# Expert products of a gated recurrence with top-k routing on one core: column halves of 64, an expert's lag, and longer weight runs

## The chip, the cores and the metric

One core of one Trainium2 chip. The metric is the device time of one execution in microseconds (us); lower is better. The kernel before was run three times: median 218.14 us, 217.22 to 218.26.

## What is computed

A gated linear recurrence over 5056 steps, 4 batches and 256 channels makes 20224 tokens. Each token goes to the best of 8 experts; an expert keeps its 80 tokens with the highest gate weight and runs a two-layer product on them. All other rows of the output are zero.

```python
sig = 1.0 / (1.0 + np.exp(-f_logit))
f = lower_bound + (1.0 - lower_bound) * sig
for t in range(S):
    h = f[:, t] * h + (1 - f[:, t]) * x[:, t];  y[:, t] = h
x = y.reshape(B * S, D)
...
logits = x @ w_gate;  expert_idx = argmax(logits);  gate_w = max(softmax(logits))
for e in range(E):
    tok_idx = tokens of e; if more than capacity = 80, the 80 with the largest gate_w
    out[tok_idx] = gate_w[tok_idx, None] * (np.maximum(x[tok_idx] @ w1[e], 0.0) @ w2[e])
```

w1 is 8 x 256 x 1024 and w2 8 x 1024 x 256, all float32.

## The kernel before

It has three stages, and one queue, SP's, issues nearly all transfers in program order.

**Recurrence.** 40 units of 512 steps and one batch each. SP loads f_logit and x of a unit (`load`, L251 and L253, 512 KB each, runs of 4 KB), ACT takes the sigmoid (L257), POOL multiplies (L261), PE turns both to channels by transposes (`to_channels`, L268), ACT makes the decay (`decay`, L278), DVE scans (`scan`, L286). The result stays on chip as `h_all`. PE also forms the gate logits (`logits`, L301): weights of 32 columns, four matmuls on the four quarters of the array, each written to its own 32 partitions of PSUM. After four units of a group ACT, PE and DVE turn the logits to tokens and take maxima (L310 to L346).

**Selection.** From the last units on: exponentials on ACT (`exponentials`, L355; the first one over all eight older groups, 1024 columns), sums by halves on POOL (`halved`, L369), the worth of each token (L379, L383), transposes and copies to candidates (`candidates`, L389 and L395), the peaks on DVE (L400). Then two small copies on ACT (L487 the last 256 candidates, L490 the last peaks), the maxima of each row on DVE (L560 to L563), ranks, and 12 matmuls (L626) that put the kept tokens in slots. `trow` holds where they lie.

**Experts.** `experts` (from L664) runs over the 8 experts. `gather` (L688 to L693) copies the 80 tokens of an expert from `h_all`, two channels at a time, on DVE, ACT and POOL together; `scaled` (L701) scales them on DVE. The weights come in 32 tiles of 512 KB, four per expert, through a ring of six (`wring`): `weights` loads a half of W1 by hidden columns (L514, two runs of 2 KB per partition) or a half of W2 by hidden rows (L518, four runs of 1 KB). The order of the tiles is sorted by the step at which they are used (`e_step`). When a tile has been used, `more` issues the next and, behind it, one clear. A clear (`clear`, L169) copies a block of zeros inside the output, DRAM to DRAM, 256 KB mostly; 22 of the 76 quarter blocks are left when the ring is full, so each of the next 22 tiles has one behind it and the last four of the 32 have none. At most eight of SP's transfers are under way, as eight semaphores take turns.

`steps` walks over 64 chunks of 128 hidden columns: `hidden` (L725) makes two matmuls for a chunk (stationary a 128 x 128 block of W1, moving the 80 tokens), and `result` (L740), six chunks later, one for the second product (stationary the 80 tokens' hidden values of a chunk, moving 256 columns of W2), accumulated over eight chunks into 80 x 256, token by row. `relu` (L734) on ACT moves four chunks at a time from PSUM. `finish` (L755) scales by the gate weight on DVE, and `scatter` (L758) on POOL writes the 80 rows to the output by an indirect transfer. Scatters wait in a list until all clears are issued; the first then waits for the clears to land.

## Time and profile before

| | |
|---|---|
| runs | 218.14 us median (217.22 to 218.26) |
| profiled execution | 217.36 us, its span 215.5 us |
| busy | PE 187.8, weight loads 158.2, DVE 150.7, ACT 131.4, POOL 139.1 us |
| moved | 80.55 MB, mean 374 GB/s; SP's queue 94.9% of the 16 engines' span |
| w_sb transfers | 32 of 512 KB, median 7.7 us from issue to landing |
| granted TensorE clock | 0.992 over the span |

The span begins with the first instruction and ends with the last; the execution's own time has some 1.9 us around it. Busy shares are means over stages with different limits, so the rows further down are taken by stretch. PEld is the weight load that goes ahead of a matmul. A matmul in f32 has two records in the trace, a transpose one. A DMA share is the mean busy share of the 16 DMA engines; it can stand a little above 1, since packets of an engine overlap.

### The profile page before, as it was taken

How to read it: one execution, taken by the hardware profiler on the slowest of the kernel's cores; microseconds unless marked ns; L12 is line 12 of the kernel's file. 1: busy time of each engine (PE TensorE's matmuls, PEld its weight loads, DVE VectorE, ACT ScalarE, POOL GpSimd, SP SyncE). 2: the span in 40 equal slices, each digit the busy share in tenths (PEclk: the TensorE clock that was granted, in tenths of full speed). 3: DMA queues.
4: the chain of work that ended last, by engine and by line, in shares of the span. 5: the costliest groups of instructions: out<-in, count | busy, mean ns of one | idle time of the engine just before them, and what ended most of it. 6: DMA issues, size and time to landing. Idle time of an engine off the chain costs nothing. (4 is left out here: it accounts for less than half of the span.)

```text
span 215.5 us, 5581 instructions
## 1 busy us (share of the span) xinstructions
PE 187.8 (87%) x1878; PEld 158.2 (73%) x1878; DVE 150.7 (70%) x479; ACT 131.4 (61%) x370; POOL 139.1 (65%) x279
## 2 busy tenths in 40 slices
PE   7888689999999999999999767798969899889980
PEld 7677478788878787878788546798857687668850
DVE  5687659999998989898989768945777524510010
ACT  4776588879888888888878623559524443611100
POOL 3484887989898989898888761049966623000741
PEclk9999999999999999999999999999999999999996
DMA  6999999999999999999999899999999999999910
GB/s 218 414 399 416 417 422 415 418 414 426 409 417 414 419 411 417 411 407 424 409 408 395 283 378 363 386 320 400 338 368 410 392 406 405 404 401 397 319 57 24
DMA packets 28825, 80.55 MB, mean 374 GB/s; under 512 B 3058, under 2 KB 11380, under 8 KB 26484
## 3 DMA queue, kind: packets, MB, share of 16 engines
q1 hardware_dynamic: 28400, 79.45, 94.9%
q0 software_dynamic: 384, 0.66, 1.0%
q8 instruction: 17, 0.28, 0.5%
q14 instruction: 20, 0.16, 0.2%
q10 hardware_dynamic: 4, 0.00, 0.0%
HBM read 78.39 MB, written 21.36 MB: 463 GB/s over the span
## 5 line engine op out<-in xcount | busy, mean ns | idle before, releaser
L261 POOL TENSOR_TENSOR x_t<-f_t,x_t 128x1024 f32<-128x1024 f32 x39 | 92.3, 2374 | 16.4 <-DMA x_t<-in_x_dram 11.0
L286 DVE TENSOR_TENSOR_SCAN h_all<-h_all,up 128x512 f32<-128x512 f32 (+1 forms) x80 | 94.7, 1242 | 7.5 <-ACT h_all L278 6.5
L278 ACT ACTIVATE h_all<-sp,nomlb 128x512 f32<-128x512 f32 (+1 forms) x80 | 50.0, 676 | 12.6 <-PE sp L268 12.5
L257 ACT ACTIVATE f_t<-f_t 128x1024 f32<-128x1024 f32 x40 | 42.4, 1061 | 9.3 <-DMA f_t<-in_f_logit_dram 9.2
L268 PE MATMUL up<-ident,x_t 128*128 128x128 f32 x320 | 42.0, 274 | 4.7 <-POOL x_t L261 4.7
L725 PEld LDWEIGHTS h_ps<-xt,w_sb 128*128 128x128 f32 x256 | 36.8, 191 | 12.5 <-DVE xt L701 3.5
L268 PE MATMUL sp<-ident,f_t 128*128 128x128 f32 x320 | 44.6, 283 | 0.1
L268 PEld LDWEIGHTS sp<-ident,f_t 128*128 128x128 f32 x320 | 35.0, 143 | 8.2 <-issue 5.5
L268 PEld LDWEIGHTS up<-ident,x_t 128*128 128x128 f32 x320 | 35.6, 141 | 6.8 <-POOL x_t L261 6.7
L725 PE MATMUL h_ps<-xt,w_sb 128*128 128x80 f32 x256 | 36.8, 269 | 4.0 <-DMA w_sb<-in_moe_w_dram 3.1
L740 PE MATMUL y_ps<-w_sb,hid 128*80 128x256 f32 x128 | 37.3, 381 | 1.3 <-DMA w_sb<-in_moe_w_dram 1.3
L693 POOL COPY xe<-h_all 128x8 uint8 x192 | 26.5, 198 | 16.4 <-issue 6.5
L301 PE MATMUL lg<-h_all,wg 128*32 128x128 f32 (+1 forms) x640 | 26.5, 282 | 5.3 <-ACT ls L310 3.9
L693 DVE COPY xe<-h_all 128x8 uint8 x256 | 20.8, 163 | 11.5 <-issue 11.4
L734 ACT ACTIVATE hid<-h_ps 128x320 f32<-128x320 f32 x16 | 7.0, 436 | 32.3 <-PE h_ps L725 32.3
L301 PEld LDWEIGHTS lg<-h_all,wg 128*32 128x32 f32 x640 | 15.4, 108 | 12.3 <-ACT ls L310 6.8
L693 ACT COPY xe<-h_all 128x8 uint8 x192 | 20.2, 193 | 5.5 <-issue 3.5
L758 POOL DMA_INDIRECT out_dram<-y,goal x8 | 7.5, 938 | 23.8 <-DMA w_sb<-in_moe_w_dram 19.7
L755 DVE TENSOR_SCALAR y<-y_ps,gsl 80x256 f32<-80x256 f32 x8 | 3.8, 477 | 22.6 <-PE y_ps L740 22.6
L183 PE MATMUL warm<-ident 128*128 128x128 f32 x128 | 17.2, 298 | 1.4 <-POOL ident masks.py:199 1.4
L183 PEld LDWEIGHTS warm<-ident 128*128 128x128 f32 x128 | 16.6, 212 | 1.5 <-POOL ident masks.py:199 1.4
L740 PEld LDWEIGHTS y_ps<-w_sb,hid 128*80 128x80 f32 x128 | 14.8, 152 | 2.2 <-issue 1.4
(126 smaller groups left out, 91.9 us busy)
## 6 DMA issues: line engine op xcount, KB each, us to landing
f_t<-in_f_logit_dram SPq DMA_DIRECT2D x40, 512.0 KB, 6.1
x_t<-in_x_dram SPq DMA_DIRECT2D x40, 512.0 KB, 6.5
w_sb<-in_moe_w_dram SPq DMA_DIRECT2D x32, 512.0 KB, 7.7
out_dram<-out_dram SPq DMA_DIRECT2D x34, 256.0 KB, 7.8
out_dram<-out_dram SPq DMA_DIRECT2D x6, 768.0 KB, 11.6
out_dram<-out_dram SPq DMA_DIRECT2D x4, 1024.0 KB, 12.4
out_dram<-zero SPq DMA_DIRECT2D x4, 256.0 KB, 8.4
out_dram<-out_dram SPq DMA_DIRECT2D x2, 512.0 KB, 7.8
```

The lines of the kernel that those rows point to most:

```text
L183: nc.tensor.matmul(warm, ident, ident, start=True, stop=True)
L257: nc.scalar.activation(s_t, s_t, ACT.Sigmoid, scale=-1.0)
L261: (nc.gpsimd if n else nc.vector).tensor_tensor(u_t, sts[n], u_t, ALU.mult)
L268: nc.tensor.transpose(at, src[n][:, r, ds(o * P, P)], ident)
L278: nc.scalar.activation(columns(n, o).rearrange("c (p r) -> c p r", r=R), sps.pop((n, o)).rearrange("c (r p) -> c p r", r=R) [:, lead(n // ...
L286: nc.vector.tensor_tensor_scan(h, h, ups.pop((n, o))[:, lead(n // B):], columns(n - B, o)[:, size(n // B - 1) - 1:] if n >= B else 0.0, AL ...
L301: nc.tensor.matmul(lgs[g][ds(r * LC, LC), b, :k], wg[:, o], h[:, r], start=o == 0, stop=o == DC - 1, skip_group_check=True)
L693: copy(xe[:, :, ds(WORD * (k + j), WORD)], pair(v - HOME))
L725: nc.tensor.matmul(HP[e, i][:, c], w[1, e, i][:, o, ds(c * P, P)], XT[e][:, o], start=o == 0, stop=o == DC - 1, skip_group_check=True)
L734: nc.scalar.activation(HID[e][:, ds(i * CH, CH)], HP.pop((e, i)), ACT.Relu)
L740: nc.tensor.matmul(YP[e], HID[e][:, c], w[2, e, c // CH][:, c % CH], start=c == 0, stop=c == FC - 1)
L758: one = nc.gpsimd.indirect_dma_start(out=out, out_offset=bass.IndirectOffsetOnAxis(ap=goal[:, ds(e, 1)], axis=0), in_=Y.pop(e), in_offset= ...
```

## The change

Six edits. W1 is loaded by halves of the 256 input channels, one run of 4 KB per partition, and `hidden(e, o)` uses one such half for all eight chunks. W2 is loaded with two hidden rows next to each other on a partition, two runs of 2 KB; so that the hidden values match, `hidden` takes every second column of W1. Each matmul of `hidden` has 64 stationary columns, two of them for the two halves of the partitions. `result` is turned: W2 is stationary, 64 output channels at a time, and the hidden values move, so that the product comes out by channel; `lift` copies it from PSUM on ACT and `across` turns it to tokens by two transposes on PE. The second product of an expert runs between the two input halves of the next; the transposes, `finish` and `scatter` come one expert later still. In the selection, the first exponential is cut in two and group 8's is taken earlier and to a tile of its own, its sum goes ahead of its choice, and the two small ACT copies stand behind the first maximum (L560) and its replacement. Pools are opened without `with` (the routing code moves one level to the left), `gsm` on the right side, and the weights of the ring stand ahead of the end of the selection in the program.

```diff
-def e_step(key, chunks, half, lag):
+def e_step(key):
     which, e, i = key
-    return e * chunks + i * half + (lag if which == 2 else 0), which
+    return 2 * (e + which - 1) + i, which
...
         elif n == LAST - 2:
-            exponentials(0, OLD)
+            exponentials(0, HALF)
         elif n == LAST - 1:
             halved(0, HALF)
+            exponentials(HALF, OLD)
+            exponentials(OLD, OLD + 1, aside=True)
...
     aside(g, 0, B - 1)
-    best = chosen(OLD)
-    exponentials(OLD, OLD + 1)
     logits(LAST)
     aside(g, B - 1, B)
+    sums(OLD, OLD + 1)
+    best = chosen(OLD)
     worth(0, 0, 2, nc.gpsimd)
     worth(2, 0, 2, nc.gpsimd)
     mark(OLD, *best, nc.gpsimd)
-    sums(OLD, OLD + 1)
...
     peaks(HALF, fresh)
-    nc.scalar.copy(cand[:, OLD * P:], fresh[:, NP * TOP:])
-    eighths = fresh[:, TOP - 1:NP * TOP:TOP]
-    last_of = consts.tile([P, NP], F32, name="last_of")
-    nc.scalar.copy(last_of, eighths)
+    gsm.release()
...
         nc.vector.match_replace(out=rest, in_to_replace=vals2[:, :TOP], in_values=fresh,
                                 imm_value=GONE)
+        nc.scalar.copy(cand[:, OLD * P:], fresh[:, NP * TOP:])
+        last_of = consts.tile([P, NP], F32, name="last_of")
+        nc.scalar.copy(last_of, fresh[:, TOP - 1:NP * TOP:TOP])
...
     def weights(which, e, i):
-        t = wring.tile([P, DC * FH], F32, name="w_sb", tag="w_sb")
+        t = wring.tile([P, F], F32, name="w_sb", tag="w_sb")
         if which == 1:
-            t = t.rearrange("p (o f) -> p o f", o=DC)
-            nc.sync.dma_start(out=t, in_=w1[e][:, ds(i * FH, FH)].rearrange(
-                "(o p) f -> p o f", p=P))
+            nc.sync.dma_start(out=t, in_=w1[e][ds(i * P, P)])
         else:
             t = t.rearrange("p (c d) -> p c d", c=CH)
-            nc.sync.dma_start(out=t, in_=w2[e][ds(i * FH, FH)].rearrange(
-                "(c p) d -> p c d", p=P))
+            nc.sync.dma_start(out=t.rearrange("p (h j) d -> p h j d", j=RUN),
+                              in_=w2[e][ds(i * FH, FH)].rearrange(
+                                  "(h p j) d -> p h j d", p=P, j=RUN))
...
+            def hidden(e, o):
+                if o == 0:
+                    for i in range(2):
+                        HP[e, i] = psh.tile([P, CH, K], F32, name="h_ps", tag="h_ps")
+                for c in range(FC):
+                    i, c = divmod(c, CH)
+                    h, r = divmod(c, RUN)
+                    for j in range(0, P, HC):
+                        at = i * FH + (h * P + j) * RUN + r
+                        nc.tensor.matmul(HP[e, i][ds(j, HC), c],
+                                         w[1, e, o][:, at:at + (HC - 1) * RUN + 1:RUN],
+                                         XT[e][:, o], start=o == 0 and c == 0,
+                                         stop=o == DC - 1, skip_group_check=True)
+                del w[1, e, o]
+                more(1)
...
+            def result(e, i):
+                if i == 0:
+                    both = psy.tile([P, 2 * D], F32, name="y_ps", tag="y_ps")
+                    YP[e] = both[:, :DC * K].rearrange("p (o k) -> p o k", o=DC)
+                    YZ[e] = both[:K, D:]
+                for c in range(CH):
+                    for o in range(DC):
+                        for j in range(0, P, HC):
+                            nc.tensor.matmul(YP[e][ds(j, HC), o],
+                                             w[2, e, i][:, c, ds(o * P + j, HC)],
+                                             HID[e][:, i * CH + c],
+                                             start=i == 0 and c == 0 and o == 0,
+                                             stop=i == 1 and c == CH - 1, skip_group_check=True)
+                del w[2, e, i]
+                more(1)
+
+            def lift(e):
+                YC[e] = mp.tile([P, DC, K], F32, name="yc", tag="yc", bufs=1)
+                nc.scalar.copy(YC[e], YP.pop(e))
+
+            def across(e):
+                yc = YC.pop(e)
+                for o in range(DC):
+                    nc.tensor.transpose(YZ[e][:, ds(o * P, P)], yc[:, o], ident)
...
             for e in range(E):
                 gather(e + 2, (0,))
+                hidden(e, 0)
+                if e > 1:
+                    across(e - 2)
+                if e > 0:
+                    result(e - 1, 0)
                 gather(e + 2, (1,))
+                done(e - 2)
+                hidden(e, 1)
+                scaled(e + 2)
+                relu(e, 0)
                 relu(e, 1)
+                if e == 0 and not again:
+                    settle()
+                if e > 0:
+                    result(e - 1, 1)
+                    lift(e - 1)
...
+            across(E - 2)
+            result(E - 1, 0)
+            done(E - 2)
+            result(E - 1, 1)
+            lift(E - 1)
+            across(E - 1)
+            done(E - 1)
```

PE, the start of the experts, before. `kept` L626 are the selection's matmuls, `warm` L183 matmuls on the identity whose result is not used, `h_ps` the first product and `y_ps` the second:

```order
L626 MATMUL kept<-put,what 16x80 x12
L183 MATMUL warm<-ident 128x128 x22
L725 MATMUL h_ps<-xt,w_sb 128x80 x12
L641 MATMUL held<-count,mates 128x2
L550 MATMUL kept<-ident,flat 80x16
L725 MATMUL h_ps<-xt,w_sb 128x80 x2
L740 MATMUL y_ps<-w_sb,hid 80x256
```

The last two rows there repeat in turn to the end. The same place after the change, up to the third expert:

```order
L631 MATMUL kept<-put,what 16x80 x12
L183 MATMUL warm<-ident 128x128 x22
L733 MATMUL h_ps<-xt,w_sb 64x80 x32
L646 MATMUL held<-count,mates 128x2
L552 MATMUL kept<-ident,flat 80x16
L733 MATMUL h_ps<-xt,w_sb 64x80 x16
L753 MATMUL y_ps<-hid,w_sb 64x80 x16
L733 MATMUL h_ps<-xt,w_sb 64x80 x16
L753 MATMUL y_ps<-hid,w_sb 64x80 x16
L733 MATMUL h_ps<-xt,w_sb 64x80 x16
L768 MATMUL y_ps<-ident,yc 80x128 x2
```

One matmul of the second product behind two of the first has become 16 behind 16, and two transposes (L768) follow the next expert's first half.

PE, the end of the program, after the change:

```order
L733 MATMUL h_ps<-xt,w_sb 64x80 x16
L753 MATMUL y_ps<-hid,w_sb 64x80 x16
L768 MATMUL y_ps<-ident,yc 80x128 x2
L753 MATMUL y_ps<-hid,w_sb 64x80 x32
L768 MATMUL y_ps<-ident,yc 80x128 x2
```

Before, seven matmuls of 256 columns stood last (L740); now 32 of 80 columns and two transposes, which the ACT copy separates.

ACT, the end of the recurrence, before (L278 are the last decays, L355 the exponentials, L310 copies of gate logits):

```order
L355 ACT_TABLE_LOAD
L355 ACTIVATE cand<-cand 128x1024
L278 ACTIVATE h_all<-sp,nomlb 128x448 x2
L310 COPY ls<-lg 128x3x112
L355 ACTIVATE cand<-cand 128x128
L310 COPY ls<-lg 128x112
```

After the change:

```order
L355 ACT_TABLE_LOAD
L355 ACTIVATE cand<-cand 128x512
L278 ACTIVATE h_all<-sp,nomlb 128x448 x2
L355 ACTIVATE cand<-cand 128x512
L355 ACTIVATE ex<-cand 128x128
L310 COPY ls<-lg 128x3x112
```

Half of the long exponential stands behind the last decays now. On SP the weight tiles keep their places in the queue, each with the same clears behind it; only the kinds change places in two pairs at the start, and the last three tiles are of W2 instead of the last two.

## Rows read from the trace of the kernel before

**Rows 1.** The page, part 4: shares of the span in the chain that ended last.

```profile
DMA 19%; PE 11%; DVE 5%; POOL 2%; POOLq 1%; issue 1%; ACT 0%; SPq 0%; DVEq 0%; ACTq 0%
```

**Rows 2.** Busy us by stretch (records), granted clock, DMA share, GB/s.

```profile
core 0: us, PE busy (x) PEld busy (x) DVE busy (x) ACT busy (x) POOL busy (x), PEclk, DMA share, GB/s
20.00:60.00 40.00, 36.17 (x452) 29.93 (x450) 34.54 (x39) 32.21 (x45) 33.84 (x17) 1.00 1.03 417
...
154.00:158.00 4.00, 3.40 (x25) 2.89 (x23) 3.61 (x35) 1.67 (x13) 2.37 (x18) 1.00 0.93 281
158.00:186.00 28.00, 25.20 (x170) 20.39 (x170) 15.04 (x156) 12.39 (x95) 13.21 (x96) 1.00 1.05 404
198.00:202.00 4.00, 4.00 (x29) 3.26 (x28) 0.35 (x1) 0.44 (x1) 2.25 (x3) 1.00 1.06 373
202.00:206.00 4.00, 4.00 (x31) 3.61 (x30) 0.48 (x1) 0.44 (x1) 3.09 (x4) 1.00 0.62 213
```

**Rows 3.** The chain in order of time: start us, duration us, what.

```profile
146.89 2.90 PE h_ps L725 x24
...
209.07 0.49 DVE y L755
```

**Rows 4.** Timeline of POOL at the end: start, duration, what, idle before it.

```profile
199.14 1.12 POOL L758 DMA_INDIRECT out_dram<-y,goal  x1 [19.68 <-DMA w_sb<-in_moe_w_dram]
200.57 0.91 POOL L758 DMA_INDIRECT out_dram<-y,goal  x1 [0.30 <-issue]
...
206.65 0.91 POOL L758 DMA_INDIRECT out_dram<-y,goal  x1 [0.30 <-issue]
209.82 0.91 POOL L758 DMA_INDIRECT out_dram<-y,goal  x1 [2.27 <-DVE y L755]
```

**Rows 5.** Groups from 145 us on: busy us, mean ns of one, idle before.

```profile
L740 PE MATMUL y_ps<-w_sb,hid 128*80 128x256 f32 x128 | 37.3, 381 | 1.3 <-DMA w_sb<-in_moe_w_dram 1.3
L725 PE MATMUL h_ps<-xt,w_sb 128*128 128x80 f32 x256 | 36.8, 269 | 4.0 <-DMA w_sb<-in_moe_w_dram 3.1 <-DVE xt L701 0.6 <-DVE found L794 0.2
...
L693 ACT COPY xe<-h_all 128x8 uint8 x172 | 18.2, 192 | 4.3 <-issue 2.3 <-DVE xt L701 1.3 <-DVE doubt L795 0.7
...
L734 ACT ACTIVATE hid<-h_ps 128x320 f32<-128x320 f32 x16 | 7.0, 436 | 32.3 <-PE h_ps L725 32.3
```

**Rows 6.** Timeline of PE: gate logits, transposes, selection (weights rows*columns, then the moving operand).

```profile
117.24 0.61 PE L301 MATMUL lg<-h_all,wg 128*32 128x112 f32 x16
...
120.12 1.02 PE L301 MATMUL lg<-h_all,wg 128*32 128x112 f32 x32
...
123.15 0.44 PE L389 MATMUL ct<-ident,gm 128*128 128x128 f32 x2
...
139.39 1.82 PE L626 MATMUL kept<-put,what 128*16 128x80 f32 x24 [0.68 <-DVE put L622]
```

**Rows 7.** Groups of PEld from 118 to 150 us: a dense load and one by every fourth column.

```profile
L389 PEld LDWEIGHTS ct<-ident,gm 128*128 128x128 f32 x8 | 1.0, 140 | 2.3 <-POOL gm L383 2.3
...
L316 PEld LDWEIGHTS lt<-ident,ls 128*128 128x128 f32 x4 | 0.6, 208 | 0.0
```

**Rows 8.** Timeline of SP: the seventh and the eighth weight tile go out.

```profile
148.94 0.37 SPq L518 DMA_DIRECT2D w_sb<-in_moe_w_dram  x1
...
151.57 0.37 SPq L514 DMA_DIRECT2D w_sb<-in_moe_w_dram  x1
```

**Rows 9.** Timeline of ACT at the last units.

```profile
118.96 1.06 ACT L355 ACTIVATE cand<-cand 128x1024 f32<-128x1024 f32 x1
119.93 1.14 ACT L278 ACTIVATE h_all<-sp,nomlb 128x448 f32<-128x448 f32 x2
```

**Rows 10.** Timeline of DVE: last scan, first maximum, second expert's tokens.

```profile
120.57 2.18 DVE L286 TENSOR_TENSOR_SCAN h_all<-h_all,up 128x448 f32<-128x448 f32 x2 [0.90 <-ACT h_all L278]
...
130.45 0.47 DVE L560 MAX8 vals<-fresh 128x8 f32<-128x288 f32 x1 [0.58 <-ACT last_of L490]
...
151.17 0.34 DVE L701 TENSOR_TENSOR xt<-xe,omlb 128x160 f32<-128x160 f32 x1
```

563 lines of the change are left out of this document (266 added, 297 removed).

## The prediction

> **What bounds the kernel now.** I read the chain that ended last, then the busy times by stretch, then each engine around the places that the chain names. The chain puts 19% of the span on transfers and 11% on PE [rows 1], so I asked in which stretch which of the two is late. From 20 to 60 us the transfers run at share 1.03 and 417 GB/s; from 158 to 186 us, where the experts run, still at 1.05, but at 404 GB/s, with PE busy 25.20 of 28 us [rows 2]. There the DMA engines have no room and PE waits for weights in short pieces. At the end it is the other way: from 202 to 206 us the DMA share is 0.62, PE is busy all 4.00 us [rows 2], and the last product is ready only when its scaling starts at 209.07 us [rows 3]. So transfers bound the experts, and PE lags behind them by some 4.5 us at the end: share 0.62 of the stretch from 202 us, at a full 1.06, puts the last weights near 204.4 us.
>
> POOL has a chain of its own there. Eight scatters, the first starting at 199.14, the next at 200.57, then every 1.21 us (206.65 is the seventh); only the eighth waits, 2.27 us, for the last product, and starts at 209.82 [rows 4]. The first cannot start before the last clear has landed, because the clears write the same rows of the output.
>
> **PE, the first product.** Before, 16 matmuls per expert with 128 stationary columns and 80 moving ones, two records each (the trace splits an f32 matmul): 24 records took 2.90 us [rows 3]; without the 269 ns of the last [rows 5] that is 114 ns from one to the next. The second product runs 256 moving columns; the two groups are busy 36.8 and 37.3 us [rows 5]. After, both products are 32 matmuls per expert with 64 stationary and 80 moving columns, in pairs on the two halves of the array. No row shows halves of 64, but the gate matmuls L301 do the same with quarters of 32: 16 records took 0.61 us and 32 took 1.02 [rows 6], so four more rounds of four cost 0.41 us, 103 ns a round of four matmuls of 112 columns. That is about the stream of one of them; the four run side by side, and their weights are loaded beside each other. For 80 moving columns the stream is in the selection matmuls L626: 24 records in 1.82 us, 76 ns each [rows 6]. I take 77 ns for a round of two halves. Bounds: 52 ns (half of the 103, if two ran as freely as four) and 152 ns (two times 76, nothing side by side). The value is nearest to L301, which has the same pattern with more groups.
>
> The halves of the first product read every second column. L316, which reads every fourth, has loads of 208 ns where a dense one (L389) has 140 [rows 7]: 68 ns more for 128 columns, 34 for 64. L725's 114 ns are more than its stream of 76, so they are the load of 128 columns, and 64 take about 57; with the 34, 91 ns beside a stream of 77: a round of 91 for that product at most.
>
> One weight tile is then 16 rounds, 1.23 us (1.46 strided). Two transposes per expert are new: two took 0.44 us with entry and exit [rows 6]; 0.4 an expert, which also covers the change of shape. An expert needs 4 x 1.23 + 0.4 = 5.3 us of PE (5.8 strided), the transfers of its four tiles and four clears 2 x 3.89 = 7.8 us: 2 x 0.524 + 2 x 0.262 MB at 404 GB/s is 3.89 us. PE stops being a bound, and the transfers decide to the end.
>
> The Trainium skill speaks against it: "TensorE: Matmul & The Clock Gate", Part 3, says that a weight load overlaps running matmuls only when the row group differs, and here both halves use all rows. By that rule a round would be about 134 ns and the sum 227.2 us (a rival, below). L725's stream at 114 ns, where load and stream one after the other would be 190, does not bear it out [rows 3, 5].
>
> **Transfers.** Bytes stay; runs double: W1 from 2 to 4 KB, W2 from 1 to 2 KB. From 198 to 202 us almost only W2 moves, at 373 GB/s: 1.41 us a tile. Loads in 4 KB runs (x, f_logit) move at 417: 1.26 us [rows 2]. I take the 0.15 us for W2's 16 tiles, 2.4 us, and nothing for W1. Bounds: 0, and 4.8 if W1 gains as much. "DMA: Bandwidth & Descriptors", Specifications, in the Trainium skill gives line rate from 512 B up; by it the term is 0 and the sum 214.7 us. The 373 against 417 speaks for a price per run.
>
> The ring of six tiles is the other source: from 154 to 158 us the share falls to 0.93 and the rate to 281 GB/s [rows 2]: (404 - 281) x 4 us = 0.49 MB, 1.2 us lost, since the seventh tile was issued at 148.94 us and the eighth at 151.57 [rows 8]. After, a tile is given back after 1.2 us of PE instead of 1.7: the seventh goes out near 147.1, the eighth near 148.4. I take 0.7 of the 1.2, as the transfers were slow there for other reasons too; bounds 0 and 1.2.
>
> **Selection, before the experts.** The exponential of 1024 columns (1.06 us) stood ahead of the last decays on ACT [rows 9]; its half is enough now, about 0.5 us, and the scan idled 0.90 us for it [rows 10]: 0.5 us earlier, nothing to 0.9. The copy of the last candidates moves behind the first maximum, which idled 0.58 us for it [rows 10]; the copy now runs beside DVE: 0.5 us. The reduction put ahead of the choice of group 8 delays POOL by 0.3 us, hidden, as DVE meets those results only later. The first expert so starts at 145.9 instead of 146.89, and this is counted in the 147.1 above, not again: the end waits for bytes.
>
> **New steps behind the last weights.** The scaled product needs a copy from PSUM on ACT (below the 436 ns of a relu of 320 columns [rows 5], 0.35 for 160), two transposes (0.45) and the scaling (0.49 [rows 3]). For the first seven experts this lies under the next expert. ACT's relus move behind both parts of a gather; its 24 copies at 192 ns mean [rows 5], 4.6 us at the most, still leave it 2 us within the 7.8.
>
> **The sum.** Of the transfers 28 of 32 tiles go before the last clear, so that lands 14/16 x 2.4 + 0.7 = 2.8 us earlier and the first scatter starts at 196.3. Eight in a row (1.43, 6 x 1.21, 0.91) end at 205.9. The last weights land near 204.4 - 2.4 - 0.7 = 201.3; 1.5 for their 16 rounds with entry, 0.4 for the copy, 0.5 for the transposes and 0.55 for the scaling make 204.2, and its scatter could start at 204.5; its turn in the row comes at 205.0. So **POOL's row of scatters ends last**, 205.9 instead of 210.73 (209.82 + 0.91): -4.8 us. All that follows is as before. The profiled execution took 217.36 us (span 215.5); the sum gives 212.6. The median of the runs shown is 218.14, 0.8 higher, so 212.6 is at the low side of what a median may be.
>
> **Rivals.**
> - *The runs cost nothing and the hole stays.* The last clear lands as before; what goes is PE's lag. Eight scatters from 199.14 end at 208.7: -2.0, **215.3 us**. For it: the engines count as full at every size. Against: 373 beside 417.
> - *The halves load one after the other.* Then a round is two loads, 114 ns, as much as L725 now. PE decides from about 104 ns: from 150.5 us, when the second expert's tokens are ready (151.17 + 0.34 - 1.0 [rows 10]), it has 30 tiles or 480 rounds, 8 x 0.4 and 1.4 to the scaled product: 209.8, against 209.56 now: +0.3, **217.6 us**, no change. Break-even is at 113 ns. Against it: four loads of 32 columns within L301's 103 ns.
> - *Slower: a load waits for the stream of its half.* 57 + 77 = 134 ns a round; 150.5 + 64.3 + 4.6 = 219.4, **+9.9 us, 227.2**. Its place is every tile of both products; it makes the kernel slower from 113 ns a round on. For it: the short rounds were seen for 32 records in a row only [rows 6], and from 20 to 60 us PE has 452 records in 40 us, 88 ns each [rows 2], so a long stream at 38 ns is not in the rows. Against: L725's 114 ns, and L301.
> - *Nothing happens:* PE and transfers only exchange places at the end and the time stays within 1 us of 217.4; the weakest, as a lag of 4.5 us stands in the rows.
>
> **How the numbers follow.** My forecast has 0.68, with 210 to 214.5 us (W1's runs gaining too, or PE a little late with strided loads); the first rival 0.14 (215.3), the second and the last 0.06 (217 to 218), the slower one 0.12 (from 219 to 227 us, by how much of it holds). The likeliest gives 212.6. The range from 210.0 to 217.0 leaves out the slower rival and some of the tails. A measurement of this kernel can tell about 0.5%, 1.1 us, from no change. Faster: forecast and first rival, 0.82; same 0.06; slower 0.12.
>
> **What would show it.** L733 and L753 in the trace at 75 to 90 ns a round; PE waiting for weights in every expert, the share at 1.03 or more from 146 to 200 us without the dip; w_sb at 410 GB/s or more when alone; the first scatter near 196 and the eighth without a wait of over 0.3 us for y. Wrong: a PE without waits and rounds over 104 ns, or a first scatter not before 198 us.

## The result, and the profile after

The changed kernel takes **215.12 us** (median of 20 runs, 214.56 to 217.05) against 217.26 (20 runs, 216.32 to 219.16) of the kernel before on the same chip: ratio 0.9899, 95% interval 0.988 to 0.9918. That is 2.1 us faster, less than half of the 4.8 us of the forecast, which put it at 212.6 us; the time lies inside the stated range of 210.0 to 217.0 and the direction is right. Ratios here and below leave out executions that took over 1.5% longer than the fastest of their kernel, so a ratio is not always that of the two medians beside it. The profiled execution of the changed kernel took 215.43 us, its span 213.6 (before 217.36 and 215.5).

The stretches that answer to [rows 2], with the one from 150 us added (the same columns):

```profile
core 0: us, PE busy (x) PEld busy (x) DVE busy (x) ACT busy (x) POOL busy (x), PEclk, DMA share, GB/s
20.00:60.00 40.00, 36.36 (x451) 29.90 (x450) 34.52 (x39) 33.64 (x46) 33.84 (x17) 1.00 1.03 418
150.00:154.00 4.00, 3.33 (x58) 3.33 (x60) 2.68 (x31) 2.47 (x24) 4.00 (x31) 0.66 1.02 380
154.00:158.00 4.00, 2.96 (x74) 2.80 (x71) 3.33 (x26) 1.17 (x3) 4.00 (x32) 0.91 1.01 301
158.00:186.00 28.00, 20.12 (x458) 17.29 (x458) 15.80 (x170) 13.35 (x105) 10.48 (x77) 1.00 1.03 410
198.00:202.00 4.00, 3.93 (x100) 3.50 (x98) 0.48 (x1) 0.88 (x2) 2.95 (x3) 1.00 0.98 376
202.00:206.00 4.00, 3.29 (x82) 2.78 (x77) 0.48 (x1) 0.45 (x2) 2.82 (x4) 1.00 0.36 113
```

PE is busy 20.12 of 28 us among the experts where it was 25.20, so it waits for weights in every expert now. The transfers run there at 410 GB/s where they had 404. The hole from 154 to 158 us is filled (share 1.01 for 0.93), yet the rate in it is 301 GB/s for 281. And what the transfers gain there they lose just before. The 14 us around the hole (the same columns), before and then after:

```profile
146.00:160.00 14.00, 12.10 (x90) 10.68 (x89) 9.35 (x96) 8.12 (x70) 11.97 (x89) 1.00 1.00 362
```

```profile
146.00:160.00 14.00, 10.12 (x222) 9.79 (x224) 9.63 (x101) 9.50 (x83) 12.58 (x95) 0.88 1.00 350
```

The products, from 145 us on, in answer to [rows 5] (busy us, mean ns of one, idle before):

```profile
L753 PE MATMUL y_ps<-hid,w_sb 128*64 128x80 f32 x512 | 22.0, 242 | 3.7 <-DMA w_sb<-in_moe_w_dram 3.5
L733 PE MATMUL h_ps<-xt,w_sb 128*64 128x80 f32 x512 | 21.7, 239 | 10.3 <-DMA w_sb<-in_moe_w_dram 8.0 <-DVE xt L706 2.3
...
L763 ACT COPY yc<-y_ps 128x160 f32<-128x160 f32 x8 | 2.3, 292 | 11.9 <-PE y_ps L753 11.9
```

They are busy 43.7 us where the old ones were 74.1: the halves do what the prediction said of them. PE at the end (start, duration, what, idle before):

```profile
197.04 1.33 PE L733 MATMUL h_ps<-xt,w_sb 128*64 128x80 f32 x32 [0.48 <-DMA w_sb<-in_moe_w_dram]
198.30 0.42 PE L768 MATMUL y_ps<-ident,yc 128*80 128x128 f32 x2
198.78 1.33 PE L753 MATMUL y_ps<-hid,w_sb 128*64 128x80 f32 x32
199.91 1.32 PE L733 MATMUL h_ps<-xt,w_sb 128*64 128x80 f32 x32
201.18 1.33 PE L753 MATMUL y_ps<-hid,w_sb 128*64 128x80 f32 x32
202.96 0.42 PE L768 MATMUL y_ps<-ident,yc 128*80 128x128 f32 x2 [0.45 <-ACT yc L763]
203.30 2.44 PE L753 MATMUL y_ps<-hid,w_sb 128*64 128x80 f32 x64
206.19 0.41 PE L768 MATMUL y_ps<-ident,yc 128*80 128x128 f32 x2 [0.45 <-ACT yc L763]
```

64 records take 2.44 us and 32 take 1.33: 16 more rounds of two halves in 1.11 us, **69 ns a round**. After the last wait for weights, at 197.04 us, PE works without a gap but for two of 0.45 us, which wait for ACT's copy of the product. And POOL's scatters, in answer to [rows 4]:

```profile
198.40 1.12 POOL L775 DMA_INDIRECT out_dram<-y,goal  x1 [22.16 <-DMA w_sb<-in_moe_w_dram]
199.83 0.91 POOL L775 DMA_INDIRECT out_dram<-y,goal  x1 [0.30 <-issue]
...
205.92 0.91 POOL L775 DMA_INDIRECT out_dram<-y,goal  x1 [0.30 <-issue]
207.47 0.91 POOL L775 DMA_INDIRECT out_dram<-y,goal  x1 [0.64 <-DVE y L772]
```

The first scatter starts 0.74 us earlier than before (199.14), the eighth 9.07 us after the first instead of 10.68. So in this pair of traces 0.74 us of the gain comes from the transfers and 1.61 from PE's lag at the end; 0.45 is lost behind the last scatter (from its end, 208.38, to the end of the span 5.22 us; before 4.77).

### The profile page after: what moved, and what is told of

Same layout as the page of the kernel before. It is cut to its first block, busy times and chain, and to the rows that moved or that the text cites. A ratio compares the mean times of both kernels' runs of the same rounds, so it can differ in the third digit from the quotient of the medians.

```text
span 213.6 us, 6897 instructions
## 1 busy us (share of the span) xinstructions
PE 176.9 (83%) x2534; PEld 151.5 (71%) x2534; DVE 150.5 (70%) x479; ACT 133.1 (62%) x379; POOL 138.9 (65%) x279
## 4 chain that ended last, share of the span: by engine, by line
DMA 41%; PE 36%; ACT 9%; DVE 4%; issue 2%; POOL 2%; SPq 1%; POOLq 1%; ACTq 0%; DVEq 0%
DMA w_sb<-in_moe_w_dram 27%; PE sp L268 12%; PE up L268 9%; PE lg L301 8%; DMA f_t<-in_f_logit_dram 7%; DMA x_t<-in_x_dram 7%; ACT h_all L278 5%; PE y_ps L753 2%; ACT ls L310 2%; PE h_ps L733 2%; PE lt L316 2%; POOL xe L698 1%; DVE at L600 1%; ACT f_t L257 1%; PE kept L631 1%
## 5 line engine op out<-in xcount | busy, mean ns | idle before, releaser
L278 ACT ACTIVATE h_all<-sp,nomlb 128x512 f32<-128x512 f32 (+1 forms) x80 | 50.0, 677 | 12.6 <-PE sp L268 12.6
L257 ACT ACTIVATE f_t<-f_t 128x1024 f32<-128x1024 f32 x40 | 42.5, 1062 | 9.3 <-DMA f_t<-in_f_logit_dram 9.3
L268 PE MATMUL up<-ident,x_t 128*128 128x128 f32 x320 | 42.1, 274 | 3.9 <-POOL x_t L261 3.5
L268 PE MATMUL sp<-ident,f_t 128*128 128x128 f32 x320 | 44.0, 280 | 1.6 <-ACT h_all L278 1.4
L268 PEld LDWEIGHTS sp<-ident,f_t 128*128 128x128 f32 x320 | 34.3, 140 | 10.1 <-issue 5.5
L733 PE MATMUL h_ps<-xt,w_sb 128*64 128x80 f32 x512 | 21.7, 239 | 10.3 <-DMA w_sb<-in_moe_w_dram 8.0
L733 PEld LDWEIGHTS h_ps<-xt,w_sb 128*64 128x64 f32 x512 | 19.5, 142 | 12.1 <-issue 5.1
L753 PE MATMUL y_ps<-hid,w_sb 128*64 128x80 f32 x512 | 22.0, 242 | 3.7 <-DMA w_sb<-in_moe_w_dram 3.5
L753 PEld LDWEIGHTS y_ps<-hid,w_sb 128*64 128x64 f32 x512 | 19.8, 143 | 6.2 <-DMA w_sb<-in_moe_w_dram 3.9
L698 ACT COPY xe<-h_all 128x8 uint8 x192 | 19.6, 193 | 5.1 <-issue 2.8
L183 PE MATMUL warm<-ident 128*128 128x128 f32 x128 | 18.0, 306 | 1.4 <-POOL ident masks.py:199 1.4
L183 PEld LDWEIGHTS warm<-ident 128*128 128x128 f32 x128 | 17.6, 222 | 1.5 <-POOL ident masks.py:199 1.4
```

What stands on the lines that cost most here:

```text
L183: nc.tensor.matmul(warm, ident, ident, start=True, stop=True)
L257: nc.scalar.activation(s_t, s_t, ACT.Sigmoid, scale=-1.0)
L268: nc.tensor.transpose(at, src[n][:, r, ds(o * P, P)], ident)
L278: nc.scalar.activation(columns(n, o).rearrange("c (p r) -> c p r", r=R), sps.pop((n, o)).rearrange("c (r p) -> c p r", r=R) [:, lead(n // ...
L698: copy(xe[:, :, ds(WORD * (k + j), WORD)], pair(v - HOME))
L733: nc.tensor.matmul(HP[e, i][ds(j, HC), c], w[1, e, o][:, at:at + (HC - 1) * RUN + 1:RUN], XT[e][:, o], start=o == 0 and c == 0, stop=o == ...
```

## The experiments

All times are medians; "before" is the kernel before in the same rounds on the same chip. The five groups ran on chips that the results number 5, 8, 9, 5 and 4. The last two columns are from the trace: when the first and the eighth scatter start, and how long the transfers took from the 10th to the 32nd weight tile's worth of bytes (counted from the DMA packets in the trace; the last 0.01 of a tile left out). A row of the table is one kernel; its trace is one execution of it, which can lie a microsecond or two from the median.

| run | kernel | chip | us | before | ratio (95%) | scatters 1, 8 | tiles 10 to 32 |
|---|---|---|---|---|---|---|---|
| first trace | before | | | 217.26 | | 199.14, 209.82 | 41.0 us |
| first result | changed | | 215.12 | 217.26 | 0.990 (0.988 to 0.992) | 198.40, 207.47 | 40.5 |
| c1 | changed | 8 | 215.80 | 217.36 | 0.992 (0.990 to 0.995) | 199.35, 208.66 | 40.2 |
| c2 | before | 8 | 217.99 | 217.36 | 1.001 (0.998 to 1.005) | 201.89, 212.60 | 42.5 |
| d1 | changed | 9 | 214.53 | 217.12 | 0.989 (0.984 to 0.993) | 197.69, 206.78 | 40.4 |
| d2 | both runs undone | 9 | 217.45 | 217.12 | 1.001 (0.998 to 1.004) | 200.45, 210.05 | 42.4 |
| d3 | quarters | 9 | 232.61 | 217.12 | 1.069 (1.065 to 1.074) | 208.24, 225.55 | |
| d4 | tail | 9 | 215.18 | 217.12 | 0.990 (0.986 to 0.994) | 198.37, 207.43 | 41.0 |
| n1 | changed, clears left out | 8 | 206.86 | 217.36 | 0.952 (0.950 to 0.955) | 167.12, 200.57 | |
| n2 | before, clears left out | 8 | 210.52 | 217.36 | 0.969 (0.966 to 0.971) | 162.97, 202.75 | |
| e1 | second matrix 1 KB | 5 | 224.35 | 221.16 | 1.022 (1.015 to 1.030) | 198.79, 216.12 | 42.1 |
| e2 | first matrix 2 KB | 5 | 223.77 | 221.16 | 1.021 (1.015 to 1.028) | 199.18, 216.64 | 41.3 |
| e3 | second matrix 4 KB | 5 | 223.46 | 221.16 | 1.020 (1.013 to 1.028) | 198.98, 215.46 | 40.8 |
| e4 | selection undone | 5 | 223.16 | 221.16 | 1.018 (1.011 to 1.024) | 198.37, 215.74 | 40.2 |
| f1 | before | 5 | 221.13 | 219.88 | 1.002 (0.997 to 1.007) | 200.72, 212.55 | 42.1 |
| f2 | both runs undone | 5 | 224.68 | 219.88 | 1.022 (1.017 to 1.027) | 201.21, 217.64 | 43.1 |
| f3 | changed | 5 | 223.63 | 219.88 | 1.018 (1.013 to 1.024) | 198.30, 214.49 | 40.7 |
| f4 | whole products | 5 | 224.52 | 219.88 | 1.018 (1.011 to 1.026) | 198.66, 216.97 | |
| g1 | early clears | 4 | 218.20 | 219.09 | 0.997 (0.994 to 1.001) | 185.03, 210.09 | |
| g2 | changed | 4 | 222.53 | 219.09 | 1.016 (1.011 to 1.021) | 197.84, 214.99 | 40.1 |

Read chips 8 and 9 apart from 5 and 4. On the first two the changed kernel is 0.8 and 1.1% faster, as in the first result; on the other two it is 1.8 and 1.6% **slower** than before, with the same first scatter. That has a cause of its own, further down.

### What the runs are worth

The first group undid one edit each. Theory A was that the bytes alone set the pace, theory B that a longer run is worth what the prediction took.

```diff
-    RUN = 2
+    RUN = 1
```

> The changed kernel with the second product's weights back in 1 KB runs (the first matrix stays in 4 KB runs, its columns then dense). Theory A (the bytes set the pace, whatever the run): the same as the changed kernel, 215.1 us within 0.3, and the expert stretch 158 to 186 us at the same 410 GB/s. Theory B (a 2 KB run saves 0.15 us a tile of the second matrix, as the prediction had it, and something else ate the gain): 14 tiles before the last clear are 2.1 us slower, first scatter near 200.5, time near 217.3.

For e2, rows of the first matrix land in two pieces:

```diff
+    GAP = 8
...
-        t = wring.tile([P, F], F32, name="w_sb", tag="w_sb")
+        t = wring.tile([P, F + GAP], F32, name="w_sb", tag="w_sb")
...
-            nc.sync.dma_start(out=t, in_=w1[e][ds(i * P, P)])
+            for_halves = bass.AP(t.tensor, t.offset, [t.ap[0], (FH + GAP, 2), (1, FH)])
+            nc.sync.dma_start(out=for_halves, in_=w1[e][ds(i * P, P)].rearrange(
+                "p (a f) -> p a f", a=2))
...
-                        at = i * FH + (h * P + j) * RUN + r
+                        at = i * (FH + GAP) + (h * P + j) * RUN + r
```

> The changed kernel with the first matrix loaded in 2 KB runs again (each row lands in two pieces, 32 bytes apart). Theory A: within 0.3 of 215.1 us. Theory B: if the 4 KB runs carried the gain that there is, up to 14 x 0.15 = 2.1 us slower, 217.2; if the run only counts up to 2 KB, no change, and then the run of the second matrix (the kernel with 1 KB runs) must show it.

And e3:

```diff
-    RUN = 2
+    RUN = 4
```

> The changed kernel with runs of 4 KB for the second matrix as well, the first product's columns then being every fourth. Theory A: within 0.3 of 215.1 us, or a little slower (up to 0.5 us) if the loads of every fourth column stretch the first product's rounds at the end, where PE is late. Theory B: another step of the run, up to 1 us faster, 214.1.

All three met the trouble of chip 5, so their times say nothing of runs: the control on that chip (f3) took 223.63. Their transfers do. From the 10th to the 32nd tile they took 42.1 us (e1) and 41.3 (e2), against 40.1 to 41.0 in seven traces with the new runs in both matrices (the changed kernel five times, e4 and d4; mean 40.4): 1.6 us for the second matrix, 0.8 for the first, one trace each; e2 lies only 0.3 us above the slowest of the seven. One more step, 4 KB for the second matrix (40.8), gave nothing. So the second matrix's run is not free, and by these two traces the first's probably isn't either. Both undone together, where time can be read:

> The changed kernel with both run lengths undone (the first matrix in 2 KB runs, the second in 1 KB), all else kept. The traces of the single edits put the first scatter 0.4 us (second matrix) and 0.8 us (first matrix) later. Theory A (the bytes nearly alone): first scatter 0.4 to 1.2 us later than in the control, 0.3 to 1.2 us slower. Theory B (0.15 us a tile for the second matrix, as the prediction had it, and as much for the first): 2.1 to 4.2 us slower than the control, and so no better than the kernel before.

Its edit is those of e1 and e2 together. 217.45 us against 214.53 of the changed kernel on the same chip, **2.9 us slower**: theory B. The same stretches, first with both runs undone, then the control:

```profile
158.00:186.00 28.00, 19.78 (x449) 17.05 (x451) 16.58 (x176) 12.69 (x101) 11.54 (x86) 1.00 1.05 395
186.00:198.00 12.00, 8.30 (x200) 7.20 (x197) 0.80 (x2) 2.21 (x7) 0.00 (x0) 1.00 1.06 392
```

```profile
158.00:186.00 28.00, 21.50 (x490) 18.57 (x490) 15.76 (x170) 13.66 (x106) 10.66 (x79) 1.00 1.03 413
186.00:198.00 12.00, 8.87 (x202) 7.46 (x199) 0.81 (x2) 2.03 (x6) 0.31 (x1) 1.00 1.03 410
```

395 against 413 GB/s with PE idle a quarter of the time in both, so the transfers decide there: 4.5% of 40 us is 1.8 us. The single packets give the price: from 158 to 186 us the median packet of 1, 2, 4 and 8 KB takes 46, 84, 159 and 309 ns in the traces of either kernel, that is some 9 ns each besides their bytes. A tile is 32 KB for each of 16 engines: 32 x 46 - 16 x 84 = 128 ns a tile for the second matrix, 16 x 84 - 8 x 159 = 72 ns for the first, 16 x 0.2 = 3.2 us in all.

The measured part of it is no smaller: with the runs undone the changed kernel has **the time of the kernel before** (ratio 1.001, 0.998 to 1.004). All that is left of the change then, halves, turned product, order and selection, is together worth nothing that this measurement tells. The traces show two parts that cancel: PE's lag is 1.1 us shorter than before (9.60 us from the first to the eighth scatter against 10.68), but the first scatter comes 1.3 us later (200.45 against 199.14). The second pair should show whether that was chance:

> The kernel before, traced on the same chip as the next two. Its first scatter was at 199.14 and at 201.89 us in two traces, the eighth 10.7 us after it in both. Under (a) (new order slows the transfers) its first scatter lies 1 us or more ahead of that of the changed kernel with the old runs; under (b) the two lie within 0.5 us.

> The changed kernel with both run lengths undone, a second time. It was 2.9 us slower than the changed kernel and equal to before. From the packets (46, 84 and 159 ns for 1, 2 and 4 KB) the runs are worth 16 x 16 x (2 x 46 - 84) ns = 2.0 us for the second matrix and 16 x 8 x (2 x 84 - 159) = 1.2 us for the first, 3.2 us in all of an engine's time. Theory A (a few tenths): 0.3 to 1.2 us over the control; theory B (the price per run): 2 to 3.2 us over it. Under (a) again no faster than before, under (b) 1.0 to 1.6 us faster than before.

It fell on chip 5, where times are governed by something else. In the traces the old runs in the new order took 43.1 us for the 22 tiles, those of before 42.1. Over all traces that is 42.4 and 43.1 against 41.0, 42.5 and 42.1: the new order seems to move the same bytes in the same runs about 0.9 us slower. With two traces against three, which overlap, this is likely and not shown; what would do it is open.

The three traces of before are not alike, and the granted clock goes with it. In c2 PE waited 2.69 us for weights behind the hole (1.32 in the first trace) and was then granted 0.50, the lower level of 1.2 GHz, for 6.8 us (stretches with the columns as above):

```profile
157.00:160.40 3.40, 1.07 (x9) 0.82 (x7) 2.34 (x19) 0.10 (x1) 1.37 (x12) 1.00 1.01 372
160.40:167.20 6.80, 6.44 (x24) 5.23 (x24) 5.08 (x59) 2.11 (x17) 5.15 (x38) 0.50 1.04 399
167.20:172.00 4.80, 4.80 (x34) 3.99 (x33) 0.93 (x7) 1.63 (x10) 0.00 (x0) 1.00 0.96 345
```

PE made 24 matmul records in those 6.8 us, 44 in the first trace, and was then busy all 4.80 us while the share fell to 0.96: from 167.2 us on PE was late among the experts, and not the transfers. f1 had 3.4 us at 0.50 from 160.5 us, the first trace none before 212. The first scatter follows: 199.14, 200.72 and 201.89 us with 0, 3.4 and 6.8 us at that level. The changed kernel had 3.4 us of it from 161.2 us in c1 and moved its 22 tiles in 40.2 us even so. Three traces are few, and nothing was tried to set the clock. But the fair pair for the new order is the first trace and d2, both at 1.00 among the experts, 41.0 and 42.4 us: 1.4 us slower, one trace each and not in the same rounds.

### The selection

> The changed kernel with the selection's edits undone (one exponential of both halves, sums and copies in their old places). The first expert should start 0.9 us later (near 146.9 us). Theory A: the six tiles of the ring are given back 0.9 us later, and engines that are full afterwards cannot make this up: 0.5 to 0.9 us slower, 215.6 to 216.0. Theory B (start of the experts hidden behind the transfers): 215.1 within 0.3.

The exponentials, sums and copies stood in their old places again (e4):

```diff
         elif n == LAST - 2:
-            exponentials(0, HALF)
+            exponentials(0, OLD)
...
-            exponentials(HALF, OLD)
-            exponentials(OLD, OLD + 1, aside=True)
...
-    sums(OLD, OLD + 1)
     best = chosen(OLD)
+    exponentials(OLD, OLD + 1)
...
```

The first expert's product began at 146.94 us, in the control on that chip (f3) at 145.75. The first scatter came at 198.37 and 198.30, and the times (223.16 and 223.63, in different rounds) don't differ either: as in theory B, more than a microsecond at the start of the experts is gone by the end. That the edit made this microsecond isn't shown, since the changed kernel itself starts its first expert at 145.75, 146.01, 146.18, 146.96 and 146.97 us in five traces. The prediction had counted this edit at nothing at the end, and nothing here speaks against that.

### What PE's gain would be without the transfers

The clears behind the weight ring left out, in both kernels (55 of 76 quarter blocks of the output stay uncleared: 21 are done before the ring, in 13 transfers of one and two of four):

```diff
+    del zeros[:]
```

> The changed kernel without the clears from the weight ring on (56 of 76 quarter blocks of the output are left uncleared), so that an expert's transfers are 4 tiles at 1.26 us = 5.0 us and no scatter waits for a clear. Theory A (the transfers set the pace and hide PE's gain): an expert then takes PE's 4 x 1.33 + 0.45 = 5.8 us, 8 x 5.8 + 4 from 146 us: about 196 us for the last product, 203 to 206 us in all. Theory B (something else than bytes holds the experts, such as the steps between the engines): no more than 3 us faster than 215.

> The kernel before without the same clears. Theory A: PE's old rounds (16 rounds of 114 ns and entries, 2.3 to 2.4 us a tile... four tiles some 7.5 us an expert) bound it: 8 x 7.5 + 3 from 146.9 us, so within 3 us of 217; the changed kernel is then about 10 us faster than this one, against 2.2 with the clears. Theory B: the two differ by about 2 us, as they do with the clears.

Both get faster, by 8.9 us (206.86 against 215.80) and by 6.8 (210.52 against 217.36). So the transfers bound both kernels with the clears in, the old one too, as long as its clock holds (c2 above). Without them PE bounds the old one without a break:

```profile
158.00:186.00 28.00, 28.00 (x202) 24.55 (x201) 18.61 (x175) 14.18 (x105) 17.77 (x101) 1.00 0.96 326
```

An expert took it 6.70 us there (its scatters from the fifth to the seventh start at 185.07, 191.78 and 198.48), not the 7.5 that I had expected: PE before was 1.1 us an expert faster than the transfers, and its lag arose only at the end, when clears no longer went between the weights. The new kernel was to be 10 us faster than the old without clears and was 3.7. Where its PE runs freely it takes 4.9 us an expert, but it does not run freely:

```profile
162.32 2.25 PE L734 MATMUL h_ps<-xt,w_sb 128*64 128x80 f32 x32 [1.78 <-DVE xt L707]
...
191.37 0.42 PE L734 MATMUL h_ps<-xt,w_sb 128*64 128x80 f32 x5 [1.07 <-issue]
...
199.29 0.42 PE L769 MATMUL y_ps<-ident,yc 128*80 128x128 f32 x2 [0.45 <-ACT yc L764]
```

It waits for the second and the fourth expert's tokens (1.77 and 1.78 us) and once for DVE's scaling (1.73 us), is granted half its clock from 162.5 to 172.8 us, as the 2.25 us for 32 records show, and stands still twice with nothing to wait for (0.36 and 1.07 us). The expectation was too simple; what it was to tell apart, transfers or something else, it did.

### The number of instructions, and the halves themselves

```diff
-    HC = P // 2
+    HC = P // 4
```

> The changed kernel with both products in quarters of 32 columns: four matmuls side by side in a round, so the same stream but twice the instructions of PE, 512 an expert. Theory I (PE has run out of instructions in the pauses: without the clears it went on 1.43 us after a fetch of 16 KB had landed, twice, and the kernel before with half or fewer instructions had no pause): from the last clear on, where no weight is waited for, pauses of 0.3 us or more in the rows of PE on any chip, the last product 2 us or more later, 217.5 to 222. Theory II (the pauses have nothing to do with the number of instructions): a round as long as now, within 0.5 us of the control.

232.61 us, 18 us slower than the control: theory I, and far beyond its range. The quarters themselves are not slow: the first expert's 128 records take the time of 64 with halves (2.44 us). Three rows of PE (start, duration, what, idle before) and a stretch:

```profile
147.47 2.42 PE L733 MATMUL h_ps<-xt,w_sb 128*32 128x80 f32 x128 [0.52 <-DVE xt L706]
...
174.07 0.89 PE L753 MATMUL y_ps<-hid,w_sb 128*32 128x80 f32 x36
...
178.25 0.77 PE L753 MATMUL y_ps<-hid,w_sb 128*32 128x80 f32 x26 [3.30 <-issue]
```

```profile
158.00:186.00 28.00, 18.25 (x652) 16.52 (x641) 13.33 (x145) 8.53 (x65) 11.85 (x89) 0.82 0.94 342
```

PE stands still for 0.76 to 3.96 us eleven times, always 256 of its instructions, or a multiple of that, behind the last such place. Each time it goes on 0.9 to 1.5 us after a packet of 16,384 bytes of its instruction queue has landed; the two pauses of n1 lie at such places too, and end 1.4 us after such a packet. So PE had used up its program. The Trainium skill, "Runtime: NRT & Kernel Launch", Instruction fetch mechanics, says that instructions come in blocks of 16 KiB, 256 of them, and that the cost of crossing into the next is mostly hidden. The trace agrees on the block; the hiding held for 256 instructions an expert beside transfers of 7.7 us (no such pause in c1 and d1), and no longer for 512. The transfers then wait for PE (342 GB/s).

The other way, whole products of 128 columns in the new order:

```diff
-    HC = P // 2
+    HC = P
```

> The changed kernel with whole products of 128 columns, one matmul where it has two (half the instructions of PE). If a round is 114 ns (the old one), PE needs 4 x 1.83 + 0.4 = 7.7 us an expert, as much as the transfers, and only its lag at the end grows, by 2 to 3 us: 217 to 218. If the loads of every second column make it 148 ns for the first product, 8.8 us an expert and PE bounds it: 224 to 226. If halves are worth nothing: 215.

On chip 5: 224.52 us against 223.63 of the control, and two of its six executions took 261.75 us at a granted clock of 0.81 over the whole of them, which I can't explain. PE near the end:

```profile
194.32 2.05 PE L733 MATMUL h_ps<-xt,w_sb 128*128 128x80 f32 x16
196.20 1.95 PE L753 MATMUL y_ps<-hid,w_sb 128*128 128x80 f32 x16
197.99 2.05 PE L733 MATMUL h_ps<-xt,w_sb 128*128 128x80 f32 x16
```

From one start to the next, 16 records of the first product take 1.88 us and of the second 1.79: 117 and 112 ns each, near the old 114, so every second column costs a whole load some 5 ns at most and not 34. PE keeps up with the transfers even so: the first scatter starts at 198.66 us, 0.36 behind the control. What the halves bring is confined to the end, and how much that is can't be read on this chip.

### The end of PE

```diff
-            across(E - 2)
             result(E - 1, 0)
+            across(E - 2)
             done(E - 2)
```

> The changed kernel with one change of order at the end: the transposes of expert 6 behind the first half of expert 7's second product, so that PE has work while ACT copies (it waited 0.45 us there). Theory T (the copy and the transposes hold the end by way of the last product): the eighth scatter starts 0.3 us earlier, not waiting for its product by more than 0.2 us; 0.3 us faster than the control. If POOL's row of scatters were the end, no change.

No gain: 215.18 against 214.53 us (intervals overlap), and the eighth scatter still waits:

```profile
207.43 0.91 POOL L775 DMA_INDIRECT out_dram<-y,goal  x1 [0.62 <-DVE y L772]
```

The first 0.45 us gap is gone, but the 64 records around it took 2.90 us, where 64 in one piece took 2.44 in the profile after; the weight loads stand still for 0.4 us in two pieces there, for nothing that the trace names. The gain was lost where it was made.

### Where two chips lose 8 us

> The changed kernel itself, as the control for the first four runs: there PE stood still in seven pauses of 0.3 to 1.1 us between 201 and 207 us, with nothing that the profile shows, and the last product then ran at half clock. Theory P (the pauses belong to the chip or the moment, not to the four edits): this kernel shows them too on such a chip, 222 to 224 us, or on a quiet chip neither, 215.1. Theory Q (each of the four edits costs 8 us): 215.1 us here while its neighbours show before at 221.

> The kernel before, for a trace on the same chip. Theory P: on a chip with pauses it has some too, but half the matmuls at the end, so fewer, 218 to 222 us; on a quiet chip 217.3. Theory Q: 217.3 without any pause.

> The changed kernel again, as the control of this group. Where the kernel before runs at 217.4 us in the same rounds, 215.1 to 215.8; where that one is at 221, theory P (pauses of PE that belong to the chip) gives 222 to 224.

> The changed kernel as control: 2.2 to 2.6 us faster than before on a quiet chip; on a chip where before is at 221, 222 to 224 with the pauses of PE between 201 and 207 us.

The controls decide for theory P: on chip 5 the changed kernel itself takes 223.63 us. PE there, at the end:

```profile
201.06 0.38 PE L733 MATMUL h_ps<-xt,w_sb 128*64 128x80 f32 x5 [0.34 <-issue]
201.81 0.36 PE L733 MATMUL h_ps<-xt,w_sb 128*64 128x80 f32 x4 [0.37 <-issue]
...
205.41 0.55 PE L753 MATMUL y_ps<-hid,w_sb 128*64 128x80 f32 x4 [1.02 <-issue]
...
209.72 3.04 PE L753 MATMUL y_ps<-hid,w_sb 128*64 128x80 f32 x64
```

Four or five matmuls, a pause, and so on, for 6.3 us; after that the granted clock is 0.50 from 206 to 210 us, and the last 64 records take 3.04 us instead of 2.44. POOL in the same run:

```profile
198.30 1.12 POOL L775 DMA_INDIRECT out_dram<-y,goal  x1 [23.54 <-DMA w_sb<-in_moe_w_dram]
...
204.60 0.91 POOL L775 DMA_INDIRECT out_dram<-y,goal  x1 [0.30 <-issue]
210.66 0.91 POOL L775 DMA_INDIRECT out_dram<-y,goal  x1 [5.15 <-DVE y L772]
```

Six scatters in a row, and the last instruction ahead of the first pause starts 2.2 us after the first one's start, and the last pause ends 8.5 us after it. In the seven traces of the new order with two halves on chips 5 and 4 (e1 to e4, f2, f3, g2) these two are 2.2 to 2.5 and 8.5 to 8.6 us, though the first scatter starts anywhere from 197.84 to 201.21 and the pauses begin some 25 instructions earlier in PE's program in e3. The kernel before feels it too on chip 5 (f1): its seventh product is scaled 8.5 us after the first scatter's start, and two scatters wait:

```profile
209.96 0.91 POOL L758 DMA_INDIRECT out_dram<-y,goal  x1 [2.04 <-DVE y L755]
212.55 0.91 POOL L758 DMA_INDIRECT out_dram<-y,goal  x1 [1.68 <-DVE y L755]
```

On chips 8 and 9 the same row runs without any pause. So the row was taken apart:

```diff
                 for key in late[:m]:
                     w[key] = weights(*key)
-                    clear_some(1)
+                    clear_some(2)
```

> The changed kernel with two quarter clears after each weight tile instead of one, so that the clears are done after some 19 of 32 tiles instead of 28 and the scatters go one by one as products become ready. The bytes are the same, so the last weights land near 203.4 us as now. Theory R (POOL's row of scatters is the end on a quiet chip, and on the other chip it is in the row that the engines stand still): no pauses of PE on any chip; the eighth scatter starts when the last product is ready, 206.4 to 207.2 us, so 0.3 to 0.8 us faster than the control on a quiet chip, 214 to 215, and 7 to 8 us faster on a chip where the control takes 223. Theory S (the pauses belong to the last instructions, wherever the scatters are; and the scatters' row hides behind PE's lag): the same as the control, within 0.3 us, on either chip.

> The changed kernel as control: 214.5 to 215.8 us where before is at 217.4, or 222 to 224 with pauses of PE where before is at 220 to 221.

On chip 4 the control took 222.53 us, with the pauses, and this kernel **218.20**, 4.3 us less. Its scatters:

```profile
185.03 1.12 POOL L775 DMA_INDIRECT out_dram<-y,goal  x1 [19.36 <-DMA w_sb<-in_moe_w_dram]
...
202.45 0.91 POOL L775 DMA_INDIRECT out_dram<-y,goal  x1 [4.55 <-DVE y L772]
206.84 0.91 POOL L775 DMA_INDIRECT out_dram<-y,goal  x1 [3.48 <-DVE y L772]
210.09 0.91 POOL L775 DMA_INDIRECT out_dram<-y,goal  x1 [2.34 <-DVE y L772]
```

Theory R for the pauses: where scatters go one by one, from 199 us on, PE has none. It was wrong on the size. The last weights land at 205.8 us, not at 203.4: without clears between them tiles arrive faster than PE gives them back, and the last three are issued from 198.58 us on, in the control (g2) from 192.95. PE's late tokens have a part in it, it seems (POOL is busy 10.29 of the 12 us from 186). Against the kernel before it is 0.997 (0.994 to 1.001): no difference. No version here beats both kernels on every chip; the early clears were not tried on a quiet one.

## Why the prediction was wrong

**PE's rounds: right.** 69 ns, forecast 77 (at most 91 for the first product); every second column costs next to nothing (f4: 117 against 112 ns for whole loads). The slower rival, with the rule of the Trainium skill's page "TensorE: Matmul & The Clock Gate" behind it (a load overlaps only where the row group differs), would have needed 134 ns; the trace, with 69 ns, does not agree with it for column halves. The serial halves (114 ns) are out too.

**That transfers decide to the end: right**, and shown by n1 and n2 and by PE's waits.

**The term for the runs: right in size, wrong in its parts.** The forecast took 2.4 us, all from the second matrix, nothing for the first. Undone, both are worth 2.9 us of time (d2), the packets say 2.0 and 1.2. Two readings behind the term were wrong. From 198 to 202 us not "almost only W2" moved: by the packets 61% of the bytes came in 1 KB and 39% in 2 KB, so 373 GB/s is the rate of a mixture. With the new runs (77% in 2 KB, 22% in 4 KB) the same stretch gives 402 GB/s (c1), not the 417 of the loads in 4 KB, so 0.15 us a tile stood for 0.10 to 0.13. And when the ring is full 21 quarter blocks are left, not 22: 27 tiles go before the last clear, 12 of the 16 of W2 among them in the new order, so that 14/16 x 2.4 = 2.1 us should have been 12/16 x 2.4 = 1.8. The Trainium skill's figure ("DMA: Bandwidth & Descriptors", Specifications: line rate from 512 B) would have made this term 0; here packets of 1 KB pay 46 ns where an eighth of an 8 KB packet is 39, and the kernel pays for it.

**The step that failed: "the last clear lands 14/16 x 2.4 + 0.7 = 2.8 us earlier".** The first scatter came 0.74 us earlier, at 198.40 instead of 196.3, and "a first scatter not before 198 us" was the prediction's own sign of being wrong; this is 2.1 of the 2.9 us that the span missed. The runs are not what was missing: undone, they put the first scatter 2.8 us later (200.45 in d2 against 197.69 in d1; 201.21 against 198.30 on chip 5), where the sum had 2.1. What failed is the rest of the step: that the transfers would otherwise go on as before, and 0.7 us better for the hole. With the old runs the new kernel's first scatter comes 1.3 us later than that of before (200.45 against 199.14) and not 0.7 earlier. The loss lies among the experts: 395 GB/s from 158 to 186 us (d2 and f2) where before has 404, at the same share of 1.05, and only from there do the new runs lead to 410: against before, 1.5% instead of the 4% that 0.15 us in every 3.89 were to bring. Packets of each size have the same median in both; their means in that stretch are 1 to 2% longer in d2 (47.3, 85.2 and 317 ns for 1, 2 and 8 KB against 46.3, 84.3 and 311). Why is open. With one undisturbed trace of before, and first scatters of the changed kernel from 197.69 to 199.35, the 1.3 us is known to about a microsecond.

The 0.7 us for the hole was not there. The seventh tile was issued at 147.38 us and the eighth at 148.49, as forecast (147.1, 148.4), and the share rose to 1.01; but from 146 to 160 us as a whole the transfers ran at 350 GB/s (354 to 369 in four more traces: c1, d1, f3, g2) and before at 362 (357 and 360 in c2 and f1). The engines were full with slow packets: in these 14 us the packets took 17% longer in all than at their median times (11% before). An issue in time fills a queue, it doesn't quicken it.

**PE's lag: 1.61 us of the forecast 1.99** (the eighth scatter 9.07 us after the first; 8.69 by the row of scatters alone). It waits 0.64 us for the last product, which is ready 3.7 us after the last weights (207.2 against 203.5) and not 2.9: PE has 64 records to go, not 32, and waits for the copy. This is the place where lag and row are near each other; d4 shows that the order of the transposes alone doesn't help.

**"All that follows is as before": off by 0.45 us.** Behind the last scatter every engine jumps over the fallback and drains; that takes 5.0 to 5.2 us in three traces of the changed kernel (the first, c1, d1), 4.5 to 4.8 in three of before.

**The first rival (215.3 us) met the number** by luck: it had the runs at nothing and the lag at -2.0. The runs are what the gain hangs on, and the lag is what the later transfers take back.

## What to carry to other kernels

Where all DMA engines count as full, look at the packets: each had some 9 ns besides its bytes here, so doubling a run of 1 or 2 KB is worth 9 or 5% of those bytes' time, and this is the only part of the change that still shows when it is taken away. A faster engine behind full transfers brings only its lag after the last byte; and before splitting matmuls to make it faster, count its instructions per microsecond, because PE ran out of program at 512 an expert. Price a transfer term against several traces of before and not one, look first at the clock that each was granted, and measure on more than one chip where the end of a kernel is a burst of small work on all engines.

## What the runs showed of the hardware

- PE's program comes in blocks of 16,384 bytes (256 instructions). With 512 instructions an expert PE stood still for 0.76 to 3.96 us at these borders, and so did the kernel without clears twice.
- On chips 5 and 4, not on 8 and 9, engines worked in short pieces from 2.2 to 8.5 us after the first of six indirect scatters in a row. Taking the row apart removed the pauses at the end. What of the scatters does it, and why on these chips, is open.
- PE's granted clock fell after waits and short work: 0.66 from 150 to 154 us in the changed kernel, behind 1.77 us in which PE waited for tokens; 0.50 from 206 to 210 in f3, behind the pauses; 0.50 from 160.4 to 167.2 in c2, behind a wait of 2.69 us for weights. In the first trace of before it was 1.00 in all the stretches shown, up to 206 us. In the changed kernel, with the transfers late, the low clock cost nothing that shows (c1); at the very end it cost 0.6 us and more (f3), and in the kernel before, among the experts, it goes with a first scatter 1.6 and 2.8 us later (f1, c2).
- Among five traces of the changed kernel the first expert started at 145.75 to 147.0 us, and the first scatter at 197.69 to 199.35, without a clear link between the two.
